# Attention and a gated feed-forward on one core: order of maxima, accumulators' combinations, and the last sections

## The chip, the cores and the metric

The kernel runs on one core of a Trainium2 chip. The metric is the device time of one execution in microseconds; a kernel's time is the median over its runs. The core's engines are TensorE (PE, matrix products; PEld is its weight load), VectorE (DVE), ScalarE (ACT), GpSimd (POOL) and SyncE (SP, which here issues the DMAs).

## The reference

The input is x with 2048 tokens of 576 columns, in float32. The reference normalizes each token and feeds the result to two branches, whose product is added to x:

```
xn = (x - mean) / sqrt(var + 1e-5)
q, k, v = heads(xn @ wqkv)                     # 32 heads of 18 columns
p = softmax(q @ k.T * 18 ** -0.5)              # over all 2048 tokens
s = heads_joined(p @ v) @ wo
g = silu((gelu(xn @ w_gate) * (xn @ w_up)) @ w_down)   # 4608 hidden rows, gelu by tanh
out = x + s * g
```

## The kernel before

**Precision.** Most products are made from operands that are split into a high and a low part (`wh`/`wl`, `ah`/`al`, `oh`/`ol`); three products of the parts take the place of one. The splits are made on ACT, POOL and DVE.

**Feed-forward.** The tokens are four blocks of 512 (`NB`, `TB`). The 4608 hidden rows are 18 groups of two 128-row tiles. One tile of one block is a *section*; there are 144, numbered n = 0 to 143. In a section `gate_up` issues 27 pairs of products (L425) into two PSUM banks `pg` and `pu`. `activate` turns them into h: ACT squares `pg` (L434) and copies `pu` to t (L438), and DVE makes the gate sums L435 (h from `pg`) and L439 (t from `pg`), which release the banks, and after ACT's tanh (L440) the sum L442. Sections from n = 139 on have no such copy, and finish h with L444 and L445. `finish` forms sums of pieces of h (`sums_a`: L460, or L463 to L465) and splits them (`cut_a`: L451 on ACT or L453, and L454).

After the two sections of a row group, `down` makes the down projection of the group by seven products of half-size blocks (`PRODUCTS`, L536), which DVE adds into seven accumulators `M` (L540). For the first five groups of block 0 it is the plain form with four products. The forms of `w_down` that the seven products need are made once (`sums_b` on POOL, L488 to L490, from the loaded `rawd`, then split into `T`), stored to DRAM (`ts`) and loaded again for later blocks. At the end of a block `combine` adds the seven accumulators into four quarters (L549 to L556), `gates` stores these to DRAM (`ys`), and new activations `xd` of the next block are loaded and cast (L151).

**Attention.** It is laid into the same sections. A *unit* is four heads of one block; there are 32, of four sections each (n = 11 to 138). A section has eight slots, each with a score pair (products `pe` L809, exponential on ACT L810) and a pair for a later unit's maxima (products `pm` L772, reduction `mx` on DVE L773). Behind a section's products come the products with the values (L826), whose sums leave PSUM by L830 and L832 (`accs`). When a unit's maxima are complete, `max_neg` reduces them once more (`nm`, L778), splits the result into `m2` (L781, L782) and transposes it (L784), `max_store` writes it to DRAM (`mxT`), and `max_end` reads it from there into two rows of the unit's `QT`, where it is subtracted inside the score products.

**Lead.** The first eleven sections (`FIRST` lists the maxima in each) have no score pairs; they make the first 40 maxima, so that the first unit can begin. In those with an odd n, three maxima stand behind the last gate product.

**Last sections.** Sections 139 to 143 have no attention. Between them stand 16 *steps* of the output projection, one for each 128 tokens: `split_o` (oh on ACT, ol on DVE L934 and L935), the products `po` (L959), `gate` (ACT L949 and DVE L950 on the loaded `yy`), the product with the gate (DVE L966, or L971 for block 3, whose quarters are still in `M`), the addition to x (L973), and the store of the row. `step` first splits the operands of the step after it. Block 3's quarters are gated in place (`tg`, L1026).

**Order.** The orders of PE and SP are those in which the code issues; a section's `hooks` are pieces of work that are issued after a given number of its 27 pairs. ACT, DVE and POOL are ordered by a planner with costs and priorities; `keep_in_program_order` fixes an instruction against others of its engine. PSUM has two banks for `pg`/`pu` ("f") and a ring of three double banks, which `pm`, `pe`, `acc`, `py`, `po` section 1 and every second one of the last sections share.

Of the kernel before, what the change touches and what calls it, by code (L numbers as in the profile page):

```python
# [39 lines left out]
NF = NB * NR * G  # L40
FIRST = (0, 0, 4, 4, 4, 4, 4, 5, 5, 5, 5)
ATT = range(len(FIRST), len(FIRST) + NU * NA)
# [4 lines left out]
ENDS = NF - len(FIRST) - NU * NA  # L47
GROUPS = (0, 4, 3, 3, 2)
PLAIN = len(FIRST) // G
# [5 lines left out]
QUARTERS = ((0, 0, 6), (0, 1, 4), (1, 0, 1), (1, 1, 5))  # L55
PIECES = ((0, 3, 7), (0, 0, 3), (1, 3, 7), (1, 0, 3))
EPS = 1e-5
GC = 0.044715
# [21 lines left out]
def kernel(ctx: ExitStack, tc: tile.TileContext, x, wqkv, wo, w_gate, w_up, w_down, out):  # L80
# [446 lines left out]
    def down(b, r, then={}):  # L527
        if b == 0 and r < PLAIN:
            return down_plain()
        (ah, al), T, M = FF["A"], FF["T"], FF["M"]  # L530
        for m, (i, k) in PRODUCTS:
            py = ring("py")
            for t in range(2):
                tt = slice(t * P, (t + 1) * P)
                for n, (h, w) in enumerate(((ah, 0), (ah, 1), (al, 0))):
                    nc.tensor.matmul(py[:, t, 0:DC], h[:, i, tt], T[:, w, k], start=n == 0, stop=n == 2)  # L536
            if r == 0:
                nc.scalar.activation(M[:, m], py[:, :, 0:DC], AF.Copy)
            else:
                nc.vector.tensor_tensor(M[:, m], py[:, :, 0:DC], M[:, m], op=ALU.add)  # L540
            for to, op, by in then.get(m, ()):
                nc.vector.tensor_tensor(M[:, to], M[:, to], M[:, by], op=op)
        if r == NR - 1:
            FF["gates"].append(b)

    def combine(one, two):

        M = FF["M"]
        one.tensor_tensor(M[:, 6], M[:, 6], M[:, 0], op=ALU.add)  # L549
        one.tensor_tensor(M[:, 6], M[:, 6], M[:, 3], op=ALU.subtract)  # L550
        one.tensor_tensor(M[:, 6], M[:, 6], M[:, 4], op=ALU.subtract)
        one.tensor_tensor(M[:, 4], M[:, 4], M[:, 2], op=ALU.add)
        two.tensor_tensor(M[:, 5], M[:, 5], M[:, 0], op=ALU.add)
        two.tensor_tensor(M[:, 5], M[:, 5], M[:, 2], op=ALU.add)
        two.tensor_tensor(M[:, 5], M[:, 5], M[:, 1], op=ALU.subtract)
        two.tensor_tensor(M[:, 1], M[:, 1], M[:, 3], op=ALU.subtract)  # L556
# [14 lines left out]
    def section(specials=(), tag="f", slots=False, tail=0):  # L571
# [53 lines left out]
    def finish():  # L625
# [8 lines left out]
        def hook(i, what, ahead="hooks"):  # L634
            FF[ahead].setdefault(i, []).append(what)

        if g == 1 and (b, r + 1) in NEXT:
            load_rawd((r + 1) % NR)
# [5 lines left out]
        elif (b, r) in FORMED:  # L644
            lead = n < ATT.start
            if g == 0:
                high_b(0)
                high_b(1)
                hook(2, lambda: low_b(0))
                hook(10, lambda: low_b(1))  # L650
                for k, i in enumerate((13, 20)):
                    hook(i, lambda k=k: t_piece(r, k, True))
                sums_a(g, h, vec if lead else pool)
                hook(12, lambda: cut_a(0, h, pool, pool, keep))
            else:
                for k, i in enumerate((2, 9)):
                    hook(i, lambda k=k: t_piece(r, 2 + k, True))
                sums_a(g, h, pool)
                cut_a(1, h, pool, pool, keep)
# [55 lines left out]
    with tc.tile_pool(name="att", bufs=1, reuse_waits="tile") as att:  # L715
# [46 lines left out]

        def max_pair(u, i):

# [5 lines left out]
            for a in range(2):  # L770
                rr = slice(HR * a, HR * a + HR)
                nc.tensor.matmul(pm[:, a], QS[u, r][rr, t * P:(t + 1) * P], KS[(u * NA + c) % KB][r][rr, :], start=True, stop=True)  # L772
            nc.vector.tensor_reduce(MX[u][:, 2 * r:2 * r + 2, t, c], pm, axis=AX.X, op=ALU.max)  # L773

        def max_neg(u, keep=lambda i: i):

            nm = att.tile([P, 4 * QD], F32, name="nm", bufs=1)
            keep(nc.vector.tensor_reduce(nm, MX[u].rearrange("p a t c -> p (a t) c"), axis=AX.X, op=ALU.max, negate=True))  # L778
            m2 = att.tile([P, 2, 2, 2, 4], F32R, name="m2", bufs=2)
            n2 = nm.rearrange("p (r a t) -> p a r t", r=2, a=2)  # L780
            nc.vector.tensor_copy(m2[:, :, 0], n2)  # L781
            nc.vector.tensor_tensor(m2[:, :, 1], n2, f(m2)[:, :, 0], op=ALU.subtract)  # L782
# [4 lines left out]
        def max_store(u):  # L787
            for q in range(4):
                qq = slice(32 * q, 32 * q + 32)
                nc.sync.dma_start(mxT[u % 2][:, qq], NM[u][qq])  # L790

        def max_end(u):

            del NM[u]
            for a in range(2):
# [65 lines left out]
        for n, m in enumerate(FIRST):  # L861
            none = [lambda: None]
            lead = [lambda s=s: max_pair(*divmod(s, NS)) for s in range(slot, slot + m)]
            section((n == 2) * 5 * none + lead + (m > 0 and n != 2) * none, "ring" if n == 1 else "f",
                    tail=3 * (m > 0 and n % G == 1))
            if slot + m >= NS > slot:
                max_neg(0, tc.keep_in_program_order)
                max_store(0)
                FF["hooks"].setdefault(10, []).append(lambda: max_end(0))
            slot += m  # L870
# [13 lines left out]
        for n in range(NU * NA):  # L884
# [15 lines left out]
            if ended:  # L900
                max_neg(um - 1)
# [4 lines left out]
            if ended:  # L906
                max_store(um - 1)
                FF["hooks"].setdefault(10, []).append(lambda v=um - 1: max_end(v))
            downs()
# [7 lines left out]
    with tc.tile_pool(name="epi", bufs=1, reuse_waits="tile") as epi:  # L917
# [3 lines left out]
        def load_wo():  # L921
            keep = tc.keep_in_program_order
            nc.gpsimd.memset(f(OW[1])[HR:P, KT, :], 0.0)
            for i, w in enumerate(OW):
                keep(nc.sync.dma_start(f(w)[:, 0:KT, :], wos[i, 0:R0, :].rearrange("(k p) n -> p k n", p=P)))
                for a in range(2 - i):
                    keep(nc.sync.dma_start(f(w)[HR * a:HR * a + HR, KT, :], wos[i, R0:D, :]))

# [23 lines left out]
        def project_o(b, j):  # L952
# [24 lines left out]
        n, outs = 0, []  # L977

# [12 lines left out]
        def step():  # L991
# [4 lines left out]
            if n + 1 < len(groups):  # L996
                load_xy(*groups[n + 1])
            if n > 1:
                store()

        for i in range(ENDS):
            section([], "ring" if i % 2 else "f")
            if i == 1:
                ready()
            downs()
            finish()
            if i == 0:
                load_wo()
                load_xy(*groups[0])
                load_xy(*groups[1])  # L1010
                todo.pop("rec")[0]()
            if 0 < i <= NU - scaled:
                scale(scaled + i - 1)
                store_scale(scaled + i - 1)
            if i < NU - scaled:
                load_scale(scaled + i)
            for k in range(GROUPS[i]):
                step()
        add, sub = ALU.add, ALU.subtract
        downs({6: ((6, sub, 3),), 0: ((6, add, 0), (5, add, 0), (5, add, 2)), 4: ((6, sub, 4), (4, add, 2)),  # L1020
               1: ((5, sub, 1), (1, sub, 3))})
        M = FF["M"]
        for i, c, m in QUARTERS:
            t = ffn.tile([P, 2, DC], F32, name="tg", tag=("h0", "h1")[c], bufs=2 - c)
            nc.scalar.activation(t, M[:, m], AF.Tanh, scale=0.25)
            nc.vector.scalar_tensor_tensor(M[:, m], t, 1.0, M[:, m], op0=ALU.add, op1=ALU.mult)  # L1026
        for k in range(TB // P):
            step()
        store()
# [28 lines left out]
```

## Time and profile before

| what | value |
|---|---|
| median of 3 runs | 2640.95 us (2639.36 to 2644.98) |
| profiled execution, its time | 2645.98 us |
| its span | 2643.9 us |
| PE busy | 2576.6 us, 97% |
| DVE busy | 2161.6 us, 82% |
| POOL busy | 1554.9 us, 59% |
| ACT busy | 1473.7 us, 56% |
| DMA | 442.87 MB, mean 168 GB/s |

The span runs from the first to the last recorded instruction of the profiled execution; the device time of the same execution contains 2.1 us more. Busy time counts an engine's instructions, and in a wait the profile names the engine and the tile that ended it. The granted clock is the share of full speed that TensorE was allowed.

### The profile page before, as it was taken

Reading aid. Unit: us, or ns where it says so; the run is one execution under the profiler, and the core shown is the slowest. Engines: PE = TensorE matmul, PEld = TensorE weight load, DVE = VectorE, ACT = ScalarE, POOL = GpSimd, SP = SyncE. Lnnn points to the kernel's source line nnn. Section 1 sums busy time; section 2 is a strip of 40 time slices with the busy share of each in tenths; the row PEclk is TensorE's granted clock in tenths of the full one; section 3 lists DMA queues with packets and bytes.
Section 4 is the critical chain, followed back from the end, with each engine's and each line's share of the span. In section 5 each row is a group of like instructions: output and inputs, shape, how many; then the busy total and the mean of one; then the engine's idle time right before and its main releaser. Section 6 shows DMA issues by size and latency. Waiting matters only on the chain.

```text
span 2643.9 us, 52874 instructions
## 1 busy us (share of the span) xinstructions
PE 2576.6 (97%) x20548; PEld 1853.5 (70%) x20548; DVE 2161.6 (82%) x2474; ACT 1473.7 (56%) x1773; POOL 1554.9 (59%) x1594
## 2 busy tenths in 40 slices
PE   9998899999989999999999999999999999999988
PEld 8887766676666666667666666666666667666777
DVE  5325789999988988999988989888888988987467
ACT  3223266666657655555666555555566555565622
POOL 2215488888888855556566565555556555555620
PEclk9999899999999999999999999999999999999989
DMA  8774265555565556666676666555566655554683
GB/s 265 261 239 133 65 173 161 165 160 156 162 174 183 165 144 160 166 162 166 167 181 169 165 167 160 158 158 155 151 151 186 163 149 154 154 150 137 189 253 122
DMA packets 407880, 442.87 MB, mean 168 GB/s; under 512 B 106700, under 2 KB 286412, under 8 KB 407632
## 3 DMA queue, kind: packets, MB, share of 16 engines
q1 hardware_dynamic: 407632, 439.50, 59.7%
q8 instruction: 163, 2.67, 0.4%
q14 instruction: 85, 0.70, 0.1%
HBM read 344.12 MB, written 95.26 MB: 166 GB/s over the span
## 4 chain that ended last, share of the span: by engine, by line
PE 86%; DVE 7%; DMA 3%; ACT 2%; POOL 1%; issue 1%; SPq 0%; POOLq 0%; ACTq 0%; DVEq 0%
PE pg L425 19%; PE py L536 14%; PE acc L826 13%; PE pu L425 12%; PE pe L809 9%; PE pm L772 8%; PE po L185 7%; DVE mx L773 2%; PE po L959 2%; PE py L523 1%; DVE m L782 1%; DMA KA<-qk 1%; DVE h L435 1%; DVE accs L832 1%; DVE h L442 1%
## 5 line engine op out<-in xcount | busy, mean ns | idle before, releaser
L810 ACT ACTIVATE pT<-pe 128x1024 f32<-128x1024 f32 x1024 | 1047.6, 1026 | 618.9 <-PE pe L809 587.3
L773 DVE TENSOR_REDUCE mx<-pm 128x2 f32<-128x1024 f32 x1024 | 1222.2, 1224 | 195.2 <-PE pm L772 181.0
L425 PE MATMUL pu<-xd,wh 64*128 64x512 f32 x2538 | 932.6, 399 | 13.6 <-DVE t L439 11.5
L425 PE MATMUL pg<-xd,wh 64*128 64x512 f32 x2538 | 931.6, 399 | 2.8 <-ACT t L438 2.8
L425 PEld LDWEIGHTS pg<-xd,wh 64*128 64x128 f32 x2538 | 472.0, 186 | 116.3 <-issue 63.9
L425 PEld LDWEIGHTS pu<-xd,wh 64*128 64x128 f32 x2538 | 472.2, 186 | 44.1 <-DVE t L439 12.8
L425 PE MATMUL pg<-xd,wl 64*128 64x512 f32 x1269 | 500.1, 394 | 0.9 <-POOL wl L115 0.9
L425 PE MATMUL pu<-xd,wl 64*128 64x512 f32 x1269 | 499.2, 393 | 0.0
L108 POOL TENSOR_SCALAR wh<-raw 128x384 fp32r<-128x384 f32 x402 | 214.2, 535 | 454.0 <-PE pu L425 319.2
L826 PE MATMUL acc<-pT,VS 128*32 128x512 f32 x4096 | 466.0, 595 | 0.0
L809 PE MATMUL pe<-QT,KA 64*128 64x512 f32 x2048 | 418.2, 399 | 22.3 <-DVE mx L773 8.6
L110 POOL TENSOR_TENSOR wl<-raw,wh 128x384 fp32r<-128x384 f32 x402 | 411.1, 1025 | 28.1
L772 PE MATMUL pm<-KA,QT 64*128 64x512 f32 x2048 | 418.9, 395 | 2.2 <-ACT pT L810 1.7
L536 PE MATMUL py<-T,ah 128*128 128x288 f32 x1876 | 383.8, 300 | 10.5 <-DVE M L540 10.1
L540 DVE TENSOR_TENSOR M<-py,M 128x576 f32<-128x576 f32 x448 | 338.9, 757 | 29.9 <-PE py L536 15.3
L536 PEld LDWEIGHTS py<-T,ah 128*128 128x128 f32 x1876 | 300.3, 189 | 65.9 <-issue 54.0
L454 POOL TENSOR_TENSOR al<-h,ah 128x512 fp32r<-128x512 f32 (+1 forms) x139 | 286.3, 2060 | 67.9 <-ACT ah L451 58.1
L826 PEld LDWEIGHTS acc<-pT,VS 128*32 128x32 f32 x4096 | 120.0, 109 | 276.7 <-issue 230.1
L809 PEld LDWEIGHTS pe<-QT,KA 64*128 64x128 f32 x2048 | 193.8, 184 | 146.2 <-DVE mx L773 33.6
L536 PE MATMUL py<-T,al 128*128 128x288 f32 x938 | 276.9, 295 | 0.0
L425 PEld LDWEIGHTS pg<-xd,wl 64*128 64x128 f32 x1269 | 236.5, 186 | 30.2 <-POOL wl L115 1.7
L425 PEld LDWEIGHTS pu<-xd,wl 64*128 64x128 f32 x1269 | 236.3, 186 | 15.4
(153 smaller groups left out, 2936.3 us busy)
## 6 DMA issues: line engine op xcount, KB each, us to landing
T<-ts SPq DMA_DIRECT2D x98, 576.0 KB
KA<-qk SPq DMA_DIRECT2D x768, 72.0 KB
T<-ts SPq DMA_DIRECT2D x98, 432.0 KB
raw<-in_B_w_gate_dram SPq DMA_DIRECT2D x144, 288.0 KB
raw<-in_B_w_up_dram SPq DMA_DIRECT2D x144, 288.0 KB
ts<-T SPq DMA_DIRECT2D x36, 576.0 KB
VS<-vs SPq DMA_DIRECT2D x128, 152.0 KB
qk<-t SPq DMA_DIRECT2D x72, 256.0 KB
```

The source lines that it names most:

```text
L108: first = nc.gpsimd.tensor_scalar(hi, raw, 1.0, 1.0, op0=ALU.mult, op1=ALU.mult)
L110: keep(nc.gpsimd.tensor_tensor(lo, raw, f(hi), op=ALU.subtract))
L185: nc.tensor.matmul(o, st, m, start=(i == 0), stop=(i == len(terms) - 1))
L425: nc.tensor.matmul(o, w[1 + wp][k][rr, c, :], xd[k][xp][rr, c, :], start=(i == 0), stop=(i == len(terms) - 1))
L454: keep(two.tensor_tensor(lo, raw, f(hi), op=ALU.subtract))
L536: nc.tensor.matmul(py[:, t, 0:DC], h[:, i, tt], T[:, w, k], start=n == 0, stop=n == 2)
L540: nc.vector.tensor_tensor(M[:, m], py[:, :, 0:DC], M[:, m], op=ALU.add)
L772: nc.tensor.matmul(pm[:, a], QS[u, r][rr, t * P:(t + 1) * P], KS[(u * NA + c) % KB][r][rr, :], start=True, stop=True)
L773: nc.vector.tensor_reduce(MX[u][:, 2 * r:2 * r + 2, t, c], pm, axis=AX.X, op=ALU.max)
L809: nc.tensor.matmul(pe[:, a], KS[(u * NA + c) % KB][r][rr, t * P:(t + 1) * P], QS[u, r][rr, :], start=True, stop=True)
L810: nc.scalar.activation(PT[u, kt][:, 2 * r:2 * r + 2, :], pe, AF.Exp, scale=SCALE)
L826: nc.tensor.matmul(ACC[u][32 * a:32 * a + 32, :], VS[(u * NA + c) % VB][:, v:v + 32], pt[:, a, :], start=first, stop=last, skip_group_chec ...
```

## The change

1. **Lead.** `FIRST` spreads the 40 maxima otherwise. In the odd sections the three last maxima keep their place on PE, but their reductions on DVE are issued after the gate sums of `activate` (list `late`).
2. **Maxima's parts.** The two operations on `m2` move from DVE to GpSimd. The transposition is issued at hook 4 of the next section, the store at hook 5, and the load into `QT` at hook 16 instead of 10.
3. **Combinations.** The eight additions among accumulators at the end of blocks 0 to 2 are issued in pairs (one on DVE, one on GpSimd) at hooks 6, 12, 18 and 24 of the next section, instead of all together. In the section that ends a block, the sums and splits of h move to hook 9 of the next one.
4. **Last sections.** The loop over the last five sections is written out, with an order by hand for ACT, DVE and POOL too. The order was: section 139, section 140, down, 4 steps, section 141, 3 steps, section 142, down, 3 steps, section 143, 2 steps, down, 4 steps. It becomes: sections 139, 140 and 141, down, 4 steps, section 142, 3 steps, down, 2 steps, section 143, 2 steps, down, 5 steps. Pieces of `T` are loaded two at each step. Four of the last combinations and the additions to x of blocks 0 to 2 go to GpSimd.

The number of matrix products is the same.

```diff
-FIRST = (0, 0, 4, 4, 4, 4, 4, 5, 5, 5, 5)
+FIRST = (0, 0, 3, 5, 3, 5, 3, 6, 4, 6, 5)
...
+COMBINED = ((6, (6, ADD, 0), (5, ADD, 0)), (12, (6, SUB, 3), (5, ADD, 2)), (18, (6, SUB, 4), (5, SUB, 1)),
+            (24, (4, ADD, 2), (1, SUB, 3)))
...
-        if r == NR - 1:
+        if r == NR - 1 and b < NB - 1:
             FF["gates"].append(b)
+            for i, one, two in COMBINED:
+                FF["hooks"].setdefault(i, []).append(lambda a=one, b=two: (combine(nc.vector, *a), combine(nc.gpsimd, *b)))
...
         for b in FF["gates"]:
-            combine(nc.vector, nc.gpsimd)
...
         FF["act"] = activate(pg, pu, g, n < ATT.stop)
+        for t in FF.pop("late", ()):
+            t()
...
+        def behind(what):
+            if (n + 1) % (NR * G) == 0:
+                hook(9, what)
+            else:
+                what()
...
-            sums_a(g, h, pool if n in ATT else vec)
-            cut_a(g, h, *((pool, pool) if n in ATT else (act, vec)))
+            behind(lambda: (sums_a(g, h, pool), cut_a(g, h, pool, pool)))
...
-            nc.vector.tensor_copy(m2[:, :, 0], n2)
-            nc.vector.tensor_tensor(m2[:, :, 1], n2, f(m2)[:, :, 0], op=ALU.subtract)
+            keep(nc.gpsimd.tensor_copy(m2[:, :, 0], n2))
+            keep(nc.gpsimd.tensor_tensor(m2[:, :, 1], n2, f(m2)[:, :, 0], op=ALU.subtract))
+            NM[u] = m2
+
+        def max_turn(u):
             mt = att.tile([P, 8 * QD], F32, name="mt", bufs=2)
-            nc.vector.transpose(mt, f(m2).rearrange("p a i r t -> p (a i r t)"))
+            tc.keep_in_program_order(nc.vector.transpose(mt, f(NM[u]).rearrange("p a i r t -> p (a i r t)")))
...
+        def max_parts(u):
+            max_neg(u)
+            for i, part in ((4, max_turn), (5, max_store), (16, max_end)):
+                FF["hooks"].setdefault(i, []).append(lambda part=part: part(u))
...
-            section((n == 2) * 5 * none + lead + (m > 0 and n != 2) * none, "ring" if n == 1 else "f",
-                    tail=3 * (m > 0 and n % G == 1))
+            late = FF["late"] = []
+            ends = 3 * (m > 0 and n % G == 1)
+            lead = [lambda s=s, l=None if s < slot + m - ends else late: max_pair(*divmod(s, NS), l) for s in range(slot, slot + m)]
...
-            nc.vector.tensor_tensor(xx, xx, t, op=ALU.add)
+            (nc.gpsimd if b < NB - 1 else nc.vector).tensor_tensor(xx, xx, t, op=ALU.add)
...
+        ctx.enter_context(tc.manual_schedule(engines={mybir.EngineType.Activation, mybir.EngineType.DVE, mybir.EngineType.Pool}))
+        h, end = last_section("f")
+        ready()
+        end()
...
+        load_wo()
+        load_xy(*groups[0])
+        todo.pop("rec")[0]()
+        load_xy(*groups[1])
...
+        h, end = last_section("ring")
+        end()
+        h1, end = last_section("f")
...
+        last_down(0)
...
+        step()
...
+        for k in range(3):
+            step()
+        h, end = last_section("ring")
+        end()
+        for k in range(3):
+            step()
+        last_down(1)
...
+        for k in range(2):
+            step()
+        h, end = last_section("f")
+        end()
+        sums_a(1, h, vec)
+        cut_a(1, h, act, vec)
+        for k in range(2):
+            step()
+        last_down(2, {6: ((vec, 6, SUB, 3),), 0: ((vec, 6, ADD, 0), (pool, 5, ADD, 0), (pool, 5, ADD, 2)),
+                      4: ((vec, 6, SUB, 4), (vec, 4, ADD, 2)), 1: ((pool, 5, SUB, 1), (pool, 1, SUB, 3))})
+        step()
```

More of the change, by code (lines that the diff above doesn't have):

```diff
@@ L862 @@
             none = [lambda: None]
[L863 to L865 removed]
+            late = FF["late"] = []
+            ends = 3 * (m > 0 and n % G == 1)
+            lead = [lambda s=s, l=None if s < slot + m - ends else late: max_pair(*divmod(s, NS), l) for s in range(slot, slot + m)]
+            if ends:
+                lead[m - ends:m - ends] = none
+            elif m:
+                lead = 5 * none + lead if n == 2 else 2 * none + lead + none
+            section(lead, "ring" if n == 1 else "f", tail=ends)
             if slot + m >= NS > slot:
[L867 to L869 removed]
+                max_parts(0)
             slot += m
@@ L997, in step @@
                 load_xy(*groups[n + 1])
+            for p in pieces[:2]:
+                p()
+            del pieces[:2]
             if n > 1:
                 store()
[L1001 to L1018, printed above, removed]
@@ L1019, with scaled_rows, last_section, end @@
-        add, sub = ALU.add, ALU.subtract
-        downs({6: ((6, sub, 3),), 0: ((6, add, 0), (5, add, 0), (5, add, 2)), 4: ((6, sub, 4), (4, add, 2)),
-               1: ((5, sub, 1), (1, sub, 3))})
+        def scaled_rows():
+            if rest:
+                scale(rest[0])
+                store_scale(rest.pop(0))
+            if rest:
+                load_scale(rest[0])
+        def last_section(tag):
+            n = FF["n"]
+            FF["n"] += 1
+            g = n % G
+            pairs, pg, pu = gate_up(tag)
+            hooks, FF["hooks"], FF["next"] = FF["hooks"], FF["next"], {}
+            for i in range(n + 1, min(n + 3, NF)):
+                if i not in FF["raw"]:
+                    FF["raw"][i] = load_gu(i % (NR * G))
+            nxt = FF["raw"].pop(n + 1, None)
+            if nxt:
+                split_gu(nxt, 0)
+                split_gu(nxt, 1)
+            for p in spread(pairs, (), 1, hooks):
+                p()
+            if nxt:
+                split_gu(nxt, 2)
+            FF["w"] = nxt
+            h = ffn.tile([P, 3 + 3 * g, TH], F32, name=f"h{g}", bufs=2 - g)
+            t1 = h[:, 0:2].rearrange("p a t -> p (a t)")
+            nc.scalar.activation(t1, pg, AF.Square)
+            nc.vector.scalar_tensor_tensor(t1, t1, 1.0 / GC, pg, op0=ADD, op1=ALU.mult)
+            nc.scalar.activation(t1, t1, AF.Tanh, scale=GC * GS)
+            def end():
+                nc.vector.scalar_tensor_tensor(t1, t1, 1.0, pg, op0=ADD, op1=ALU.mult)
+                nc.vector.tensor_tensor(t1, t1, pu, op=ALU.mult)
+            return h, end
@@ L1025 @@
             nc.scalar.activation(t, M[:, m], AF.Tanh, scale=0.25)
-            nc.vector.scalar_tensor_tensor(M[:, m], t, 1.0, M[:, m], op0=ALU.add, op1=ALU.mult)
-        for k in range(TB // P):
-            step()
+            nc.vector.scalar_tensor_tensor(M[:, m], t, 1.0, M[:, m], op0=ADD, op1=ALU.mult)
+            if m == 4 or m == 5:
+                step()
+                step()
         store()
```

68 lines of the change are left out of this document (41 added, 27 removed).

## The prediction

> **What bounds the kernel now.** I read the page's busy times and its chain, then the waits of TensorE (PE), then the stretches in which PE is idle or its clock is low.
>
> ```profile
> span 2643.9 us, 52874 instructions
> PE 2576.6 (97%) x20548; PEld 1853.5 (70%) x20548; DVE 2161.6 (82%) x2474; ACT 1473.7 (56%) x1773; POOL 1554.9 (59%) x1594
> PE 86%; DVE 7%; DMA 3%; ACT 2%; POOL 1%; issue 1%; SPq 0%; POOLq 0%; ACTq 0%; DVEq 0%
> ...
> PE pu L425 <- DVE t L439: 11.5, 4, 2.9
> PE py L536 <- DVE M L540: 10.1, 3, 9.1
> PE pe L809 <- DVE mx L773: 8.6, 6, 2.1
> PE pe L809 <- DVE accs L832: 7.5, 11, 1.3
> PE po L959 <- DVE ol L934: 5.6, 2, 4.6
> ```
>
> PE is 97% busy and carries 86% of the chain. The change leaves the number of matmuls as it is, so time can come only from PE's idle gaps and from its clock. The waits (total us, times, longest) name five kinds of gap, all released by VectorE (DVE): four at the ends of lead sections, some seventeen short ones (mx and accs), mostly where attention units or token blocks end, and two long ones in the last sections. The windows place them (start:end, length; busy time of PE, PEld, DVE, ACT, POOL; granted clock, DMA share, GB/s):
>
> ```profile
> 206.00:336.00 130.00, 114.75 (x850) 95.26 (x848) 90.92 (x106) 42.26 (x75) 61.75 (x53) 0.92 0.37 97
> 753.00:800.00 47.00, 40.10 (x289) 25.88 (x287) 37.30 (x41) 25.48 (x31) 42.07 (x41) 0.93 0.57 165
> 1366.00:1402.00 36.00, 31.82 (x250) 20.25 (x244) 31.00 (x32) 21.34 (x25) 28.68 (x30) 1.00 0.83 225
> 1982.00:2018.00 36.00, 31.73 (x230) 21.86 (x231) 29.68 (x29) 19.46 (x22) 26.31 (x26) 0.95 0.71 203
> 2504.00:2644.00 140.00, 117.37 (x846) 107.93 (x844) 97.60 (x147) 31.45 (x45) 19.71 (x23) 0.91 0.62 195
> 235.00:239.00 4.00, 2.45 (x12) 1.99 (x14) 2.19 (x4) 2.08 (x4) 0.97 (x1) 0.50 0.52 110
> ```
>
> PE is idle for 15.3 us of the lead's 130, 6.9, 4.2 and 4.3 us around the three block ends, and 22.6 us of the last 140. The last row shows the second loss: behind a lead gap the granted clock is 0.50, so matmuls take twice as long. Lead and tail average 0.92 and 0.91: 8% of 114.75 is 9 us and 9% of 117.37 is 10.6 us of full-speed work lost beside the idle time.
>
> **The lead.** At the end of sections 3, 5, 7 and 9 three maxima stand behind the last gate product; DVE reduces them before the two gate sums (L435, L439) that free PSUM for the next section.
>
> ```profile
> 231.81 3.49 DVE L773 TENSOR_REDUCE mx<-pm 128x2 f32<-128x1024 f32 x3 [1.96 <-PE pm L772]
> 235.81 0.68 DVE L439 TENSOR_TENSOR t<-t,pg 128x512 f32<-128x512 f32 x1
> 232.53 0.59 ACT L438 ACTIVATE t<-pu 128x512 f32<-128x512 f32 x1
> 236.55 0.79 PE L425 MATMUL pu<-xd,wh 64*128 64x512 f32 x1 [2.88 <-DVE t L439]
> ```
>
> The copy t is ready at 232.53 + 0.59 = 233.12; DVE reaches L439 at 235.81 only because of the reductions. With the sums ahead, L439 can end near 233.12 + 0.68 = 233.8, and PE starts near 233.9–234.2 instead of 236.55: 2.5 us at each of three ends, 7.5 us. The reductions then run beside the next section's products. If the short gap no longer lowers the clock, three quarters of the 9 us go too; I take 6 of them.
>
> The Trainium skill, "TensorE: Matmul & The Clock Gate", section "HAM oscillation — how this bites in real kernels", asks for no PE idle gaps above about 3.4 us. By that rule the clock should not have fallen behind 2.88 us, and the 6 us would not be gained. The trace disagrees, since its clock was 0.50 behind this gap.
>
> The fourth end, section 9, closes the first unit's maxima. The copy and subtraction of m2 move to GpSimd (POOL), where the new order puts three sums of the next weight (L488 to L490) and a weight's split ahead of them. DVE's transposition, ahead of all reductions of section 10, now waits for POOL.
>
> ```profile
> 332.39 1.43 POOL L488 TENSOR_TENSOR tsum<-rawd 128x576 f32<-128x576 f32 x1 [6.89 <-DMA rawd<-in_B_w_down_dram]
> 335.17 0.82 POOL L490 TENSOR_TENSOR tsum<-rawd 128x288 f32<-128x288 f32 x1
> ```
>
> These sums waited 6.89 us for the load of rawd, which stood on SP behind the mxT stores, which wait for DVE. At hook 5 the stores no longer hold SP up there, so the load can start earlier; the next raw loads now stand ahead of the stores instead, whose readers have a section to spare. With an early load 1.43 + 1.43 + 0.82 = 3.7 us of sums still stand ahead of m2, and DVE stands still for 2 to 5 us with five reductions and the next gate sums behind it. I give this end no gain of its 2.88 us and charge 1 us more; bounds +5 and −5. Lead: 7.5 + 6 − 1 = **12.5** (6 to 18).
>
> **Unit ends (32).** Here DVE's two small operations on m2 can be held up while POOL works.
>
> ```profile
> 1675.42 0.21 DVE L778 TENSOR_REDUCE nm<-mx 128x16 f32<-128x64 f32 x1
> 1676.46 0.97 DVE L781 CAST m<-nm 128x16 fp32r<-128x16 f32 x1
> 1677.46 0.94 DVE L782 TENSOR_TENSOR m<-nm,m 128x16 fp32r<-128x16 f32 x1
> 1678.57 0.65 DVE L832 TENSOR_TENSOR accs<-acc,accs 128x512 f32<-128x512 f32 x1
> 1675.96 2.41 POOL L110 TENSOR_TENSOR wl<-raw,wh 128x384 fp32r<-128x384 f32 x2
> 1679.14 0.25 DVE L857 RECIPROCAL sums<-sums 128x16 f32<-128x16 f32 x1
> L464 POOL TENSOR_TENSOR h<-h,h 128x256 f32<-128x256 f32 x64 | 47.2, 738 | 0.0
> L463 POOL TENSOR_TENSOR h<-h,h 128x512 f32<-128x512 f32 x64 | 82.0, 1281 | 132.6 <-DVE m L781 94.1 <-DVE h L442 38.4
> L110 POOL TENSOR_TENSOR rest<-raw,rest 128x128 fp32r<-128x128 f32 x1 | 0.5, 468 | 0.0
> L108 POOL TENSOR_SCALAR rest<-raw 128x128 fp32r<-128x128 f32 x1 | 0.3, 297 | 0.3 <-DMA raw<-in_A_wqkv_dram 0.3
> ```
>
> Sixteen elements take DVE 0.9 us beside POOL's split; the sum accs behind them comes late, and PE waits for it. These waits on accs hold 7.5 us, each at most 1.3, and some of them belong to block ends; without DVE's two operations I take **4** of them as gained (0 to 7.5). For POOL I extrapolate the form rows: 256 more elements add 1.281 − 0.738 = 0.543 us, so 16 elements cost about 0.2–0.25 us. The nearest rows have 128 elements (0.297 and 0.468); the bound above is 1.28. In the new order, m2's copy stands behind L463 and its subtraction behind L464: ready 1.28 + 0.25 + 0.74 + 0.25 = 2.5 us after the gate sum L442. DVE gets to the transposition after nm (0.21), accs (0.65), a reciprocal (0.25) and one reduction (3.49 / 3 = 1.2) plus waiting for its product: 2.3 to 2.8 us. That is nearly level, and three PSUM buffers absorb some tenths. The QT load, now at hook 16, has whole sections before its unit. The loss case is a rival below.
>
> **Block ends (3).** The four additions of accumulators that stand together on DVE are spread over hooks 6, 12, 18 and 24.
>
> ```profile
> 777.62 2.29 DVE L549 TENSOR_TENSOR M<-M 128x576 f32<-128x576 f32 x1
> 780.52 2.00 POOL L553 TENSOR_TENSOR M<-M 128x576 f32<-128x576 f32 x1
> ```
>
> The first took 2.29 us beside POOL's work, where 512 columns take 0.68 elsewhere (L439), and reductions stood behind it. Spread, each should delay one reduction by about 1 us or less. Of 15.4 us idle, the wait for the casts of xd and the drawn-out loads stay. I take **4** (−3, if POOL's spread additions at 2.00 delay casts and splits, to +10).
>
> **The tail.** Before, the first accumulation of the second last block waits 9.1 us:
>
> ```profile
> 2516.81 7.74 DMA yy<-ys
> 2527.52 0.82 PE L536 MATMUL py<-T,ah 128*128 128x288 f32 x2 [9.07 <-DVE M L540]
> 2533.71 14.86 PE po L959 x112
> 2603.35 0.60 ACT L434 ACTIVATE h<-pg 128x512 f32<-128x512 f32 x1 [0.67 <-PE pg L425]
> 2607.83 0.42 DVE L465 TENSOR_TENSOR h<-h 128x256 f32<-128x256 f32 x1
> 2608.28 1.27 ACT L451 ACTIVATE ah<-h 128x1280 fp32r<-128x1280 f32 x1 [0.28 <-DVE h L465]
> 2610.10 1.48 DVE L454 TENSOR_TENSOR al<-h,ah 128x1280 fp32r<-128x1280 f32 x1
> 2608.83 0.68 DVE L934 TENSOR_TENSOR ol<-KA,oh 128x512 fp32r<-128x512 f32 x1
> ```
>
> The load of yy lands late, the gate's scaling on DVE waits for it, and M L540, which frees the PSUM ring, is queued behind. Written out, two whole sections run between this load's issue and its use: the 9.07 us go, and of the 10.6 us of lost clock I put half, 5 us, on this gap. The 4.6 us for ol near the end come from DVE's last combinations, four of which move to POOL; about 3 us go. Of the other 22.6 − 9.1 − 4.6 = 8.9 us of idle time I take 2, for the order between sections and steps. Gains: 9 + 5 + 3 + 2 = 19.
>
> A new gap stands against this. After section 143 two steps run on PE, 14.86 / 4 = 3.7 us each. The first has its operands; the second's split (oh on ACT, ol on DVE) is queued by hand behind that section's ah and al. From the Square to the end of L465 it is 2607.83 + 0.42 − 2603.35 = 4.9 us; ah 1.27, al 1.48 and ol 0.68 make 8.3, and a small last piece follows. Less one step of 3.7, PE waits about 5 us, and half clock behind it costs 2. Tail: 19 − 7 = **12** (0 to 20). Moving twelve additions of xx to POOL costs PE nothing, unless POOL and DVE hinder one another (rival). The other moves have cover: sums and splits behind a block's end have the next section, and the loads of wo two sections.
>
> **Sum.** 12.5 + 4 + 4 + 12 = 32.5 us. From the profiled execution's 2645.98 us (2.1 outside its span) that gives 2613.5. That execution is 5.0 above the median of the runs, 2640.95; the same gain from the median gives **2608.5**.
>
> **Rivals.** *Better than the sum* (2594 to 2602): block ends give 10, lead 18. For: idle time there is 15.4 and 15.3 us. Against: two of the releasers, xd and the fourth lead end, are untouched or worse.
>
> *The tail's gain is lost* (2620 to 2626): ACT, DVE and POOL follow a fixed order there, where one late yy or T stops everything behind it. An addition of 576 columns takes 1.43 on POOL (L488's row), so twelve hold POOL for 17 us. If DVE can't run beside them, the 12 us are gone. For it: DVE's 0.94 for 16 elements, ending with POOL's split. The Trainium skill, "SBUF — State Buffer", section "SBUF: two separate sides", calls the port which DVE and GpSimd share an exclusive lock for a whole instruction; the trace agrees at 1677.46. Against: POOL is busy for 19.71 us of those 140.
>
> *Slower, by POOL's m2* (2645 to 2665): if each of the two small operations costs POOL 1.28 us, m2 is ready 4.6 us after L442, and the transposition holds DVE by 1.8 us with seven reductions behind it. PE is late by about 1 us at each of 32 ends, 32 us, and the half clock may follow. It loses the 4 us too: 2608.5 + 36 = 2644.5 and above. It decides from about 1.2 us for an operation. Against: the 0.297 row.
>
> *The planner's order hides the gain* (2636 to 2645): each freed wait is replaced by the next engine's. Little speaks for it, since the lead's order is fixed by hand.
>
> **How the numbers follow.** Forecast 0.56, better 0.12, tail lost 0.18, slower 0.10, no change 0.04. A measurement of this kernel tells about 0.2%, 5.3 us. Faster 0.56 + 0.12 + 0.18 = 0.86, same 0.04, slower 0.10. The range takes in the better case, the forecast and the lost tail with some of the unit cost: 2594 to 2632.
>
> **What would show it.** Right: lead waits on t L439 fall from 2.9 to under 1 us with a granted clock of 0.9 or more behind three of them; no 9 us wait in the tail, but one near 5 us on ol after section 143; m2 rows on POOL near 0.25 us. Wrong: m2 rows of a microsecond and PE waits on mx at every unit's end; POOL's 1.43 rows in the tail with DVE idle beside them; a low clock in the lead without a gap.

## The result, and the profile after

The changed kernel takes 2615.32 us (median of 4 runs, 2612.9 to 2617.26), the kernel before 2642.01 us (4 runs, 2639.36 to 2644.98): a ratio of 0.9898, 95% interval 0.9881 to 0.9915. The forecast was 2608.5 us, within 2594 to 2632. The changed kernel's profiled execution took 2614.18 us. First the head of its page (span, busy times, the chain's shares), then what PE waited for (total us, times, longest):

```profile
span 2611.7 us, 52872 instructions
PE 2560.9 (98%) x20548; PEld 1858.5 (71%) x20548; DVE 2110.4 (81%) x2386; ACT 1470.5 (56%) x1770; POOL 1607.8 (62%) x1685
PE 89%; POOL 4%; DMA 3%; DVE 2%; ACT 1%; issue 1%; SPq 0%; POOLq 0%; DVEq 0%; ACTq 0%
...
PE po L974 <- DVE ol L949: 9.5, 7, 3.3
PE po L974 <- ACT oh L948: 7.5, 3, 3.1
PE pe L825 <- DVE mx L776: 6.9, 13, 1.0
PE py L538 <- DVE yy L981: 4.7, 1, 4.7
PE pu L427 <- POOL xd L153: 3.8, 2, 2.4
PE pm L774 <- DVE mx L776: 2.8, 2, 2.6
```

DVE's share of the chain fell from 7% to 2%. The waits on t (11.5 us), M (10.1) and accs (7.5) are gone from the head of the list. In their place stand the steps of the output projection, `po` waiting for ol and oh.

Since the order of sections is the same, the two profiles can be laid side by side at the ACT row that ends each section (the Square of pg, 144 rows). Between these rows:

| stretch | before, us | after, us | gain | forecast |
|---|---|---|---|---|
| up to section 0 | 203.9 | 203.3 | 0.6 | 0 |
| lead, 0 to 11 | 142.6 | 129.2 | 13.4 | 12.5 |
| units, 11–35, 39–70, 74–107, 110–138 | 1937.9 | 1921.3 | 16.7 | 4 |
| block ends, 35–39, 70–74, 107–110 | 210.7 | 202.7 | 8.0 | 4 |
| tail, 138 to the end | 148.7 | 155.2 | −6.5 | 12 |

The gains add up to 32.25 us, the difference of the spans of these two executions. The medians differ by only 26.7 us: the execution profiled before is 4.0 us above its kernel's median, the one profiled after 1.1 us below. The sum was forecast as 32.5, but two of its terms were far off, in opposite directions.

**The lead** as its DVE and PE rows show it at the end of section 3 (start, us, engine, line, operation; idle time before it), with the window that answers to 235:239 of before:

```profile
232.43 0.69 DVE L437 SCALAR_TENSOR_TENSOR h<-h,pg 128x512 f32<-128x512 f32 x1 [1.74 <-ACT h L436]
233.04 0.68 DVE L441 TENSOR_TENSOR t<-t,pg 128x512 f32<-128x512 f32 x1
233.63 3.48 DVE L776 TENSOR_REDUCE mx<-pm 128x2 f32<-128x1024 f32 x3
...
233.77 0.49 PE L427 MATMUL pu<-xd,wh 64*128 64x512 f32 x1 [0.40 <-DVE t L441]
...
234.00:238.00 4.00, 4.00 (x36) 3.30 (x36) 4.00 (x5) 0.25 (x1) 0.00 (x0) 1.00 0.64 146
```

The gate sums run first, the three reductions behind them, and PE's gap is 0.40 us instead of 2.88. PE is busy for the whole window at a granted clock of 1.00, where it had 0.50. At section 9 the first unit's transposition waits for POOL, as forecast:

```profile
303.43 1.43 POOL L490 TENSOR_TENSOR tsum<-rawd 128x576 f32<-128x576 f32 x1
307.90 0.20 POOL L789 CAST m<-nm 128x16 fp32r<-128x16 f32 x1
309.25 0.21 DVE L795 STREAM_TRANSPOSE mt<-m 128x32 f32<-128x32 f32 x1 [2.33 <-POOL m L790]
310.63 0.50 PE L774 MATMUL pm<-KA,QT 64*128 64x512 f32 x2 [2.63 <-DVE mx L776]
```

The sums of the next weight (303.43 and on) stand ahead of m2 on POOL; DVE stands still for 2.33 us and PE for 2.63.

**Unit ends.** The groups of the two operations on m2, before on DVE, after on POOL (count, then busy us and mean ns):

```profile
L782 DVE TENSOR_TENSOR m<-nm,m 128x16 fp32r<-128x16 f32 x32 | 39.0, 1220 | 1.1
L781 DVE CAST m<-nm 128x16 fp32r<-128x16 f32 x32 | 9.4, 293 | 0.0
```

```profile
L790 POOL TENSOR_TENSOR m<-nm,m 128x16 fp32r<-128x16 f32 x32 | 7.1, 222 | 0.0
L789 POOL CAST m<-nm 128x16 fp32r<-128x16 f32 x32 | 6.3, 197 | 0.0
```

Before, the subtraction of 16 elements took DVE 1.22 us on average, not only at the unit that the prediction quoted. Its rows at the first two units of the kernel before, with what POOL ran beside the second, show why:

```profile
320.89 0.17 DVE L782 TENSOR_TENSOR m<-nm,m 128x16 fp32r<-128x16 f32 x1
382.87 1.27 DVE L782 TENSOR_TENSOR m<-nm,m 128x16 fp32r<-128x16 f32 x1
382.83 1.27 POOL L463 TENSOR_TENSOR h<-h,h 128x512 f32<-128x512 f32 x1 [1.38 <-DVE m L781]
```

At the first unit POOL is idle and the subtraction takes 0.17 us. At all 31 others it runs beside an instruction of POOL and ends just behind it, at the second at 384.14 against 384.10. On POOL the two operations take 0.20 and 0.22 us, as extrapolated.

**The tail.** The 9.07 us gap is gone. Twelve gaps of 0.4 to 4.7 us, 22.8 us together, stand between 2501 and 2595 us. What SP waited for in the tail, and rows of POOL, SP, ACT and PE around the first of them:

```profile
SPq L957 <- DMA out_dram<-xx: 55.1, 12, 8.2
SPq L707 <- POOL on L700: 19.7, 2, 12.5
...
2491.54 0.51 POOL L110 TENSOR_SCALAR wh<-raw 128x384 fp32r<-128x384 f32 x1 [15.97 <-DMA raw<-in_B_w_up_dram]
...
2497.18 1.75 POOL L700 TENSOR_TENSOR on<-on,od 128x512 f32<-128x512 f32 x1
2498.90 0.78 POOL L462 TENSOR_TENSOR h<-h 128x256 f32<-128x256 f32 x1
...
2506.70 2.95 POOL L456 TENSOR_TENSOR al<-h,ah 128x1280 fp32r<-128x1280 f32 x1
2509.60 1.43 POOL L988 TENSOR_TENSOR xx<-xx,yy 128x576 f32<-128x576 f32 x1
2510.99 1.30 POOL L700 TENSOR_TENSOR on<-on,od 128x512 f32<-128x512 f32 x1
...
2512.32 1.38 SPq L707 DMA_DIRECT2D on<-on  x4
2514.20 0.37 SPq L957 DMA_DIRECT2D yy<-ys  x1
...
2517.28 0.69 ACT L964 ACTIVATE th<-yy 128x576 f32<-128x576 f32 x1 [5.40 <-DMA yy<-ys]
2521.61 0.40 PE L974 MATMUL po<-woh,oh 128*128 128x288 f32 x1 [3.03 <-ACT oh L948]
```

Two scalings L700 stand on POOL, and SP's stores L707 wait for them twice. The first, 12.5 us, ends with the scaling at 2497.18, which stood behind the split of the next weights; POOL had itself waited 15.97 us for their load. Then POOL works off the sums and splits of sections 140 and 141 (2498.90 to 2509.6), an addition to x and the second scaling; the store at 2512.32 waited the other 7.2 us for it. The next loads of xx, yy and T are queued behind these stores: the load of yy at 2514.20 lets ACT's th start at 2517.28, the next oh stands behind th in the order by hand, and PE waits 3.03 us for oh.

### The profile page after: what moved, and what is told of

Same layout as the page of the kernel before. It is cut to its first block, busy times and chain, and to the rows that moved or that the text cites. A ratio compares the mean times of both kernels' runs of the same rounds, so it can differ in the third digit from the quotient of the medians.

```text
span 2611.7 us, 52872 instructions
## 1 busy us (share of the span) xinstructions
PE 2560.9 (98%) x20548; PEld 1858.5 (71%) x20548; DVE 2110.4 (81%) x2386; ACT 1470.5 (56%) x1770; POOL 1607.8 (62%) x1685
## 4 chain that ended last, share of the span: by engine, by line
PE 89%; POOL 4%; DMA 3%; DVE 2%; ACT 1%; issue 1%; SPq 0%; POOLq 0%; DVEq 0%; ACTq 0%
PE pg L427 20%; PE acc L842 17%; PE py L538 14%; PE pu L427 12%; PE pe L825 9%; PE pm L774 9%; PE po L187 7%; PE py L525 1%; DMA raw<-in_B_w_up_dram 1%; PE po L974 1%; DVE mx L776 1%; POOL wl L112 1%; POOL al L456 0%; DMA wol<-wos 0%; POOL wh L110 0%
## 5 line engine op out<-in xcount | busy, mean ns | idle before, releaser
L456 POOL TENSOR_TENSOR al<-h,ah 128x512 fp32r<-128x512 f32 (+1 forms) x142 | 292.2, 2058 | 52.6 <-ACT ah L453 41.1
```

The lines of the kernel that those rows point to most:

```text
L456: keep(two.tensor_tensor(lo, raw, f(hi), op=ALU.subtract))
```

## The experiments

**The reductions ahead of the gate sums again** (`lead_ahead`).

```diff
-            lead = [lambda s=s, l=None if s < slot + m - ends else late: max_pair(*divmod(s, NS), l) for s in ...]
+            lead = [lambda s=s, l=None: max_pair(*divmod(s, NS), l) for s in ...]
```

> The changed kernel with the new distribution of the lead's maxima, but the three last reductions of a section issued ahead of its gate sums again. Theory (the order of DVE's work makes the lead's gain): PE waits 2 to 3 us at four ends and the clock falls, 10 to 14 us slower, 2625 to 2630 us. Rival (the other distribution, or the transposition's place, brings the gain): under 4 us slower.

Measured: 2629.90 us (ratio to before 0.9951, 0.9935 to 0.9966), 14.6 us slower than the changed kernel; the lead takes 145.5 us instead of 129.2. Of its profile the largest wait of PE, and DVE at the end of section 3:

```profile
PE pu L427 <- DVE t L441: 15.2, 4, 3.8
...
233.87 3.48 DVE L776 TENSOR_REDUCE mx<-pm 128x2 f32<-128x1024 f32 x3
237.27 0.68 DVE L441 TENSOR_TENSOR t<-t,pg 128x512 f32<-128x512 f32 x1
```

L441 is behind the reductions again and PE waits 3.8 us at four ends. The order makes the lead's gain, not the distribution: without the order this lead is 2.9 us longer than before (142.6).

**m2 back on DVE** (`m2_dve`).

```diff
-            keep(nc.gpsimd.tensor_copy(m2[:, :, 0], n2))
-            keep(nc.gpsimd.tensor_tensor(m2[:, :, 1], n2, f(m2)[:, :, 0], op=ALU.subtract))
+            keep(nc.vector.tensor_copy(m2[:, :, 0], n2))
+            keep(nc.vector.tensor_tensor(m2[:, :, 1], n2, f(m2)[:, :, 0], op=ALU.subtract))
```

> The changed kernel with the two operations on m2 back on DVE, right behind nm; transposition, store and load stay at hooks 4, 5 and 16. From section 11 to 138, outside the block ends, the changed kernel is 16.7 us faster than before, 0.45 us or more at every unit's end. Theory 1 (DVE was held at m2 while POOL worked, and the reductions were late): these 14 to 17 us come back, 2629 to 2632 us. Rival (the later place of transposition and stores brought the gain): 2615 to 2620 us.

Measured: 2642.92 us (ratio 1.0, 0.9991 to 1.0009), 27.6 us slower than the changed kernel and outside both expectations: nothing is left of the gain over the kernel before, though the lead keeps its part (126.6 us). In its profile the stretches of units are 26.1 us longer than in the changed kernel's. Its DVE groups and PE's largest wait:

```profile
L789 DVE CAST m<-nm 128x16 fp32r<-128x16 f32 x32 | 37.2, 1162 | 1.1
L790 DVE TENSOR_TENSOR m<-nm,m 128x16 fp32r<-128x16 f32 x32 | 22.5, 704 | 1.1
...
PE pe L825 <- DVE accs L848: 24.0, 30, 2.3
```

The two take 1.87 us per unit on DVE, with accs behind them, and PE waits at 30 ends. The stretches of units take 1947.4 us here, 1921.3 in the changed kernel and 1937.9 before. So 16.7 us come back, as theory 1 said (14 to 17), and 9.5 us more are lost than before the change, since m2 stands elsewhere among POOL's sums, as one unit's end shows (DVE and POOL):

```profile
1054.59 1.23 DVE L789 CAST m<-nm 128x16 fp32r<-128x16 f32 x1
1055.86 0.66 DVE L790 TENSOR_TENSOR m<-nm,m 128x16 fp32r<-128x16 f32 x1
...
1054.51 1.28 POOL L465 TENSOR_TENSOR h<-h,h 128x512 f32<-128x512 f32 x1 [6.86 <-DVE h L444]
1055.75 0.73 POOL L466 TENSOR_TENSOR h<-h,h 128x256 f32<-128x256 f32 x1
```

The copy ends at 1055.82, with POOL's first sum (1055.79), and the subtraction at 1056.52, with its second (1056.48). Before, POOL's first sum was released by DVE's copy in most units (94.1 us of its waits in the row of the prediction), and only the subtraction was held: the two took 1.51 us per unit on DVE. The 0.35 us more at each of 32 units, 11 us, fit the further 9.5; no run tests this order by itself.

**The additions together** (`combine_together`): `combine` with its eight additions called in `gates` again, the lines with `COMBINED` in `down` left out.

> The changed kernel with the eight additions among accumulators at the end of blocks 0 to 2 issued all together again, with the stores of the block's quarters. Between the ends of sections 35 and 39, 70 and 74, 107 and 110 the changed kernel takes 76.5, 74.3 and 51.9 us, the kernel before 81.0, 73.6 and 56.1. Theory (spreading the additions makes that gain, their waits on DVE being the source): 6 to 9 us slower over the three places, 2621 to 2624 us. Rival (the gain there comes from the sums and splits moved to hook 9 or from m2 leaving DVE): under 3 us slower, 2615 to 2618 us.

Measured: 2622.04 us (ratio 0.9921, 0.9906 to 0.9935), 6.7 us slower than the changed kernel. The three places take 77.0, 75.2 and 55.6 us, 5.1 us more than 202.7. PE waits 2.1 to 2.2 us for mx once at each block end again. That is less than the 6 to 9 us expected, and the ratio's interval overlaps that of the changed kernel. Of the third block end's gain 3.7 of 4.2 us go, of the first one's only 0.5 of 4.5: there the spread isn't what gained. `m2_dve` takes 80.4 us at the first, near the 81.0 before, which speaks for m2 leaving DVE; no run tests it alone.

The clock moves these stretches too. The first takes 76.3 to 77.0 us without a half-clock stretch (one in which the granted clock is 0.50) and 78.2 to 78.4 with one, in eleven profiles of the same code there; the middle one 73.0 to 73.1 and 74.3 to 74.5. The kernel before had two half-clock stretches at the first, none at the middle and one at the third; the changed kernel's profile has one at the middle alone. So its loss of 0.7 us there is that of one execution.

**The tail as before** (`tail_old`): the loop over `ENDS` and its steps in place of the written-out sections.

> The changed kernel with the loop over the last five sections as before the change, the last section's sums and splits included; the lead, the maxima's parts and the block ends stay changed. Theory (the rewritten tail costs 6.5 us): 2607 to 2611 us, and 148 to 150 us from the end of section 138 to the end. Rival (the tail gains 12 us as predicted): 2625 us and more.

Measured: 2607.37 us (2602.39 to 2608.02; ratio 0.9855, 0.9835 to 0.9875), 8.0 us faster than the changed kernel; 148.1 us behind section 138. The rewritten tail loses. An earlier form of this kernel (`tail_before`) left out the sums and splits of section 143, so its 2604.19 us say nothing of this tail.

**The additions to x on DVE, and yy loaded ahead of xx** (`xx_dve`, `yy_first`).

```diff
-            (nc.gpsimd if b < NB - 1 else nc.vector).tensor_tensor(xx, xx, t, op=ALU.add)
+            nc.vector.tensor_tensor(xx, xx, t, op=ALU.add)
```

> The changed kernel with the twelve additions to x (L988) back on DVE. Theory P (POOL's additions are what costs in the tail: they hold up DVE's subtractions, 0.7 to 1.0 us longer in a third of their rows, and end late, so the stores and the loads behind them start late): 2608 to 2611 us. Theory Q (the chain store, load of xx, load of yy on SP's queue and the fixed order of ACT bind, and POOL's additions only ride along): 2613 to 2616 us.

```diff
-            for t, a in zip(XY[b, j], (x, ys)):
+            for t, a in list(zip(XY[b, j], (x, ys)))[::-1]:
```

> The changed kernel with yy loaded ahead of xx in each step. On SP the load of xx waits for the store that frees its buffer (55.1 us in 12 waits), with the load of yy queued behind it, and ACT's th, ahead of the next oh, waits for yy. Theory Q (that chain makes the 1 to 3 us gaps before po): 2607 to 2611 us, with most of those gaps gone. Theory P (POOL against DVE): 2614 to 2616 us.

Measured: 2612.68 us (ratio 0.9895, 0.9878 to 0.9913) and 2612.27 us (0.9883, 0.9868 to 0.9898). Neither differs from the changed kernel's 0.9898 beyond the intervals, and both lie between the two expectations. Behind section 138 they take 155.9 us (in a profiled execution 6.2 us above its kernel's median) and 153.5 us against 155.2. Neither theory's cause is enough alone: in both, SP still waits over 21 us for L700.

**The scaling of rows later** (`rows_later`).

```diff
+        load_scale(rest[1])
         h1, end = last_section("f")
-        scaled_rows()
...
         step()
-        while rest:
-            scaled_rows()
         for k in range(3):
             step()
         h, end = last_section("ring")
         end()
+        for u in rest:
+            scale(u)
+            store_scale(u)
```

> The changed kernel, with the scaling of the last two units' rows (multiplication L700 on POOL, store L707 on SP) moved from behind sections 141 and the first step to behind section 142; both rows are loaded ahead of section 141. In the profile after, SP waits 19.7 us in two waits (12.5 the longest) for L700, which stands on POOL behind the sums and splits of two sections, and the loads of xx and yy are queued behind those stores. From the end of section 138 to the end of the span it is 148.7 us before the change, 155.2 after. Theory R (this stall of SP makes the gaps of the first four steps): that stretch shortens by 4 to 8 us, 2607 to 2611 us. Rival S (ACT's fixed order alone, th ahead of oh): under 2 us, 2613 to 2616 us.

Measured: 2610.82 us (ratio 0.9873, 0.9856 to 0.9889), 151.2 us behind section 138, 4.1 less: at the lower edge of theory R, with an interval that overlaps that of the changed kernel. The wait for L700 is gone, but the next one of the same kind stands in its place:

```profile
SPq L957 <- POOL xx L988: 12.4, 1, 12.4
```

The load of yy now waits for POOL's addition to x, which holds yy's buffer and is queued behind the same sums and splits (it starts at 2507.08 there, and the load of yy at 2508.58).

**The splits earlier** (`split_early`): `ready(1)`, which splits the operands one step further on, called ahead of section 143 and of `last_down(2)`.

> The changed kernel, with the next step's split (oh on ACT, ol on DVE) issued ahead of section 143 and ahead of the last down projection, instead of behind ah and al and behind the accumulations. Theory (the gaps of 3.06 and 0.97 us behind section 143 and of 1.57 and 3.31 us among the last steps come from this order): the two first gaps and at least one of the others go, 5 to 9 us with the half clock behind them, 2606 to 2610 us. Rival (these gaps are set by other work, such as POOL's combinations that hold DVE): at most 3 us.

Measured: 2615.13 us (ratio 0.9891, 0.9875 to 0.9907), no gain; 153.0 us behind section 138. The gaps at section 143 changed their name:

```profile
PE py L538 <- DMA T<-ts: 3.1, 1, 3.1
```

The steps right behind section 143 no longer wait, but the down projection behind them does, for pieces of T that SP issued late; of the waits among the last steps one of 3.1 us is left. The expectation's gain was not there.

**The old tail with other loads first** (`old_xy_first`): `tail_old` with the two first loads of xx and yy ahead of `load_wo`, and the first unit's m2 on DVE.

> The changed kernel with the old tail (2607.4 us), with the first two loads of xx and yy ahead of the loads of wo, and the first unit's m2 on DVE. Theory: the 8.4 us gap in front of the second last block's products comes from yy landing behind 10 us of wo; with yy first the gap falls to under 3 us, 5 to 8 us with its clock; the first unit's wait of 2.6 us for POOL goes too, 2.5 to 3.5 us with its clock: 2596 to 2601 us. Rival (the gap is set by something else that the planner puts ahead of the accumulation on DVE): 2603 to 2606 us.

Measured: 2605.34 us (ratio 0.9851, 0.9833 to 0.9869). The time lies in the rival's range, and the gap fell from 8.4 to 6.5 us only; the theory that yy's landing alone sets it falls, and what else the planner puts ahead there was not followed up. The lead takes 126.6 us, 2.6 less than after.

**All mended, without and with the additions to x on DVE** (`new_all`, `new_all_dve`): `rows_later`, `yy_first`, `split_early`, all four pieces of T at the first step, and the first unit's m2 on DVE; then L988's counterpart on DVE too.

```diff
-            for p in pieces[:2]:
-                p()
-            del pieces[:2]
+            for p in pieces:
+                p()
+            pieces.clear()
```

> The changed kernel with its tail mended: rows' scaling behind section 142, yy loaded ahead of xx, all four pieces of T at the first step behind a down projection and ahead of that step's loads, the next split ahead of section 143 and of the last down projection, and the first unit's m2 on DVE. Singly these were worth 4.1, 1.7 and 2.2 us of the tail's 155.2 us; the split turned the gap into a wait for T, which the earlier pieces should end. Theory (the tail's losses are queues in a fixed order, each of which can be moved): 142 to 147 us behind section 138, and 3 us less in the lead: 2599 to 2605 us. Rival (each mended wait is replaced by the next, DVE held beside POOL): 150 us and more, 2607 to 2611 us.

> The kernel new_all (2603.6 us, 145.5 us behind section 138) with the additions to x of blocks 0 to 2 on DVE. What is left of its waits at section 143 is 6.8 us in three waits of the down products for DVE's yy (L982), and DVE's small piece of oh takes 1.4 us beside POOL's addition where it takes 0.3 elsewhere. Theory P (POOL's additions hold DVE up, which shows once the queues are mended): the three waits shrink, 141 to 144 us behind section 138, 2599 to 2602 us. Theory Q (DVE's own nine further microseconds cost as much as the holding did): 145 to 148 us, 2603 to 2606 us.

Measured: 2603.64 us (ratio 0.9851, 0.9836 to 0.9865) and 2597.32 us (2594.7 to 2599.16; ratio 0.9817, 0.9804 to 0.983). Behind section 138 they take 145.5 and 140.4 us, the second 8.3 less than the kernel before. It is 18 us faster than the changed kernel and the fastest of all. Its waits of PE behind section 138, and the group of DVE's small piece of oh in the changed kernel, in `new_all` and in `new_all_dve` (each in a fence of its own):

```profile
PE po L975 <- DVE ol L950: 4.9, 4, 2.4
PE py L538 <- DVE yy L982: 3.4, 2, 2.4
PE py L538 <- DVE M L542: 1.7, 2, 1.4
```

```profile
L950 DVE TENSOR_TENSOR oh<-KA,oh 64x128 fp32r<-64x128 f32 x16 | 13.6, 848 | 0.5
```

```profile
L951 DVE TENSOR_TENSOR oh<-KA,oh 64x128 fp32r<-64x128 f32 x16 | 14.5, 908 | 0.4
```

```profile
L951 DVE TENSOR_TENSOR oh<-KA,oh 64x128 fp32r<-64x128 f32 x16 | 7.0, 438 | 0.5
```

DVE's 64x128 subtraction takes 0.85 and 0.91 us on average with the additions on POOL, 0.44 without them. In single rows of these three profiles it is 1.38 to 1.42 us beside an addition of POOL and 0.28 or 0.29 where POOL is idle. Moving the same twelve additions gained 6.3 us (2603.64 − 2597.32) where the queues were mended, 5.1 of them behind section 138, and 2.6 us, within the intervals, where they were not: a cost that hides behind a larger one.

## Why the prediction was right or wrong

The kernel came out 6.8 us above the forecast, inside the range. That the sum of the terms is met so closely, 32.25 against 32.5, is luck: the units gained 12.7 us more than forecast, the block ends 4.0 more, and the tail 18.5 less.

**Lead: right, by its own steps.** 13.4 us against 12.5. The gap at each end is 0.40 where "PE starts near 233.9–234.2" said about that. The clock did not fall behind these gaps, so that term came too. The fourth end was charged 1 us net; the rows show DVE's wait of 2.33 us for POOL, PE's gap of 2.63 and one half-clock stretch behind it. Against the 126.6 us with the first unit's m2 on DVE (`old_xy_first`, `new_all`) its whole price is 2.6 us here, but 1.2 us in `rows_later`, where the same gap has no half-clock stretch behind it (127.8 us).

**Unit ends: right mechanism, wrong size.** 16.7 us against 4 (bounds 0 to 7.5). The step that failed is the bound: it was taken from PE's waits on accs, 7.5 us. At 26 of the 28 unit ends of these stretches, also where the waits show nothing, the section is about 0.4 us or more shorter after, and up to 1.6 us where a wait was listed. PE's records before show idle time of only 9.5 us in these stretches, and after 1.4 us, so about half of the gain was never idle time in them. The row that would have warned of it was L782's group, 39.0 us in 32, where 32 × 0.17 = 5.4 us would do with POOL idle. The rival by POOL's m2 needed about 1.2 us for an operation; at 0.20 and 0.22 the transposition waits for POOL at only 5 of 32 units, 5.9 us in all.

**Block ends: right sign, but the gain was twice the forecast.** 8.0 us against 4, inside −3 to 10. Two of three gain 4.5 and 4.2, the middle one loses 0.7; its wait for xd's casts is 2.4 us there with half clock behind it. Of the 8.0 us the spread itself makes 5.1; the term had nothing for m2 or for the clock, which was at half in three stretches before and in one after.

**Tail: wrong.** −6.5 us against +12, outside its bounds of 0 to 20. The removed gap of 9.07 us and the new one behind section 143 (3.06 + 0.97 where 5 was forecast) came as worked out. The 4.62 us for ol near the end, of which 3 were to go, are still there as 1.57 and 3.31. The step that failed most is "The other moves have cover": the sums and splits of sections 140 and 141 on POOL have time for themselves, but a scaling L700 and the additions to x queue behind them, and SP's loads behind those. Another scaling waits behind a weight's split. The second step is that twelve additions on POOL cost PE nothing: moving them back gained 6.3 us once the queues were mended. With the queues mended and the additions on DVE the new order of sections does gain: 148.7 − 140.4 = 8.3 us in `new_all_dve`, against 12. The rival "the tail's gain is lost" named in-order engines and the shared port, at 2620 to 2626 us; it took the 12 us for lost where 18.5 were, and had the place only in part, for SP's queue was not in it. The gain at the units is what kept the time below it.

**The clock and the port.** The Trainium skill, "TensorE: Matmul & The Clock Gate", section "HAM oscillation — how this bites in real kernels", sets its limit at gaps of about 3.4 us. The runs here disagree as before: the gap of 2.63 us at 308.0 is followed by a half-clock stretch at 311.1, one of 2.42 at 1349.1 by one at 1352.2; of before's gaps of 2.10 and 2.12 us at block ends the first kept a clock of 1.00 and the second did not. The first two stand alone, while the gap of 2.88 us in the prediction has another of 0.70 just ahead of it. The Trainium skill, "SBUF — State Buffer", section "SBUF: two separate sides", describes the lock between DVE and GpSimd. The same subtractions on DVE agree with it: m2's takes 1.27 us beside POOL's sum and 0.17 with POOL idle, the small piece of oh 1.40 and 0.28.

## What to carry to other kernels

An operation of 16 elements took 1.27 us here beside another engine's work and 0.17 alone; read an operation's mean duration against its size, and not the waits alone, since a gain of 16.7 us showed as only 8 us less idle time. When work goes to an idle engine, list what else waits in that engine's queue and which DMA queue waits on it: here 10.7 us of sums and splits on POOL held a store for 7.2 us, the store held SP, and SP held the next steps' loads. Mend such queues together: singly, the mends here were worth 4.1 us of the tail or less, and two of them only gave a wait another name. And compare terms of a few microseconds over several executions, for the clock alone moved the same code by 1 to 2 us.

## What the runs showed of the hardware

In the profiles of before and after, the granted clock fell to half behind 15 of the 16 gaps of 2 us and more, for 3.41, 6.83 or 10.24 us, and behind no single gap of 1.6 us or less. Other runs show that neither length decides by itself. The gap of 2.6 to 2.7 us at the end of the lead had no half-clock stretch behind it in `rows_later` (2.69 us), one of 3.41 us in the changed kernel (2.63) and one of 6.83 us in `split_early` (2.66); a single gap at the first block end had one at 1.41 us in `yy_first` and none at 1.42 us in the changed kernel.

A copy of 16 elements costs POOL 0.20 us and a subtraction 0.22, though the smallest row that the prediction had was 0.30 at 128 elements. DVE's copy of the same 16 elements, with one input only, was held as well as its subtraction: 1.22 to 1.24 us in 28 of its 32 rows in `m2_dve`, beside POOL's first sum, and 0.16 or 0.17 us in 27 of 32 before the change, where POOL's sum began only behind it.
